# Batch 0's softmax over states computed a second time with tokens on partitions, in a mixed attention and feed-forward kernel on one core

## The chip, the cores and the metric

The kernel runs on 1 core of one Trainium2 chip. The metric is device time in microseconds (us). One execution of each kernel is also taken by the hardware profiler; its trace gives the span and every instruction's start and end. The engines are named as in the trace: PE (TensorE matmul) and PEld (its weight loads), DVE (VectorE), ACT (ScalarE), POOL (GpSimd) and SP (SyncE, which issues most DMAs).

## The reference, cut to what matters

```python
# x: (8, 8, 512, 64) = batch, head, token, width; state: (8, 8, 32, 64)
scores = x @ state.T / 8            # token by state; softmax over the 32 states
xread = softmax(scores) @ state
scores2 = state @ x.T / 8           # state by token; softmax over the 512 tokens
sread = softmax(scores2) @ x
y = concatenate([xread, sread])     # 544 rows of 512 per batch
out = y + relu(layernorm(y) * g @ w_ch1) @ w_ch2      # w_ch1: 512 x 2048
```

Both softmaxes use the same 512 x 32 scores per head, once normalised over the states and once over the tokens.

## The kernel before, in words

Every float32 matrix is split into two float16 halves and each product is made of three or four half products (`TERMS`). The feed-forward part of batch 0 goes directly with the weights, four units of 512 hidden columns; batches 1 to 7 and the state rows go through a Strassen scheme (`products`, lines L895, L905, L953). For each batch, `attention(b)` computes the scores with the states on partitions (a row of the scores tile is one state of one head, its columns are tokens), and from them two things. The softmax over tokens runs along a row: maximum `mB`, exponentials `eB`, their halves `eb`, a DMA transpose to `ebT`, and `read_state` on PE, which gives `sread`. The softmax over states needs the states along the free dimension: `softmax_first` turns the scores in 32 x 32 blocks on DVE (`nc.vector.transpose`, STREAM_TRANSPOSE in the trace) into `ts`, `softmax_rest` subtracts the maximum `mA`, takes the exponential, sums into `dA` and multiplies by the reciprocal, and `numerators` turns the result back on DVE into `ef` and splits it into the halves `ea`. `ea` is the moving operand of the hidden layer's products: `state_products` makes `matrix` (weights times state), and `first_products` (batch 0) multiplies `matrix` with `ea`.

Batch 0 is worked in two parts of 256 tokens (`parts = 2`), and its attention stands among the preparation of the weights: loading, unpacking (`words`: tiles `raw` and `sums`), sums of squares, scales, centring and splitting into `w1c` and `w2h` for four units. That preparation keeps DVE, ACT and POOL occupied and PE partly; PE is given `WARM` = 135 matmuls of ones with ones (`half<-ones`) whose result nobody uses.

The order of all work is written out by hand in `PLAN`: streams of operations are recorded first, and `issue` then emits them in PLAN's order. Each engine runs its own instructions in that order. Stream 177 is the warming matmuls, 1 is `attention(0)`, 2, 7, 12 and 20 are `weights1` of units 0 to 3, 3, 8, 13 and 21 `state_products`, 4, 9, 14 and 22 `first_products`. All recorded operations carry line L187 (the helper `do`), so tiles tell them apart.

PSUM pools matter here: `banks()` is one buffer of two banks (`ps_a`, bufs=1), shared by everything that asks for it (the scores, `read_state`'s result, the next batch's sums of squares and scores); `accumulator()` has four buffers of one bank. In SBUF, `quad` has two buffers, shared by `eB`, `ts`, `ef` and the `part` tiles of batch 0's second layer, which a POOL-issued DMA adds into `xr`.

Of the kernel before, what the change touches and what calls it, by code (L numbers as in the profile page):

```python
# [15 lines left out]
ALU = mybir.AluOpType  # L16
# [144 lines left out]
)  # L161
WARM = 135


class Later:
# [36 lines left out]
def moe_attention(ctx: ExitStack, tc: tile.TileContext, x, state, g_ln, w1, w2, out):  # L202
# [176 lines left out]
    def attention(b):  # L379
# [117 lines left out]
        def softmax_first(s):  # L497
            if b > 0:
                for g in range(G):
                    yield do(scores, g, ps[:, g], sT, xT)  # L500
# [577 lines left out]
```

## Time and profile before

| | us |
|---|---|
| median of 3 runs | 632.14 (631.65 to 632.55) |
| the profiled execution | 632.65 |
| its span | 630.5 |
| PE busy | 614.7 (97% of the span) |
| PEld busy | 483.5 |
| DVE busy | 488.7 (78%) |
| ACT busy | 375.3 (60%) |
| POOL busy | 242.5 (38%) |

The profiled execution has 2.15 us around its span, and is 0.51 us above the median. Busy shares are averages over the whole span: the first 80 us, in which the weights are prepared, and the rest differ.

### The profile page before, as it was taken

What the parts mean: (1) busy time and instruction counts of PE and PEld (TensorE: products, weight loads), DVE (VectorE), ACT (ScalarE), POOL (GpSimd) and SP (SyncE); (2) the same over time, 40 slices, a digit from 0 to 9 for tenths busy, and PEclk for the clock granted to TensorE, in tenths of its full rate; (3) what the DMA queues carried; (4) which work ended last, traced back from release to release, by engine and by line L of the source; (5) the groups of instructions that cost most, each with busy time, mean ns of one, the idle gap of its engine ahead of it and who ended that gap; (6) DMA issues with size and microseconds to landing.
All of it is one profiled execution on the core that took longest, in us unless ns stands there. A gap on an engine that the chain in (4) does not pass through costs nothing.

```text
span 630.5 us, 16626 instructions
## 1 busy us (share of the span) xinstructions
PE 614.7 (97%) x6906; PEld 483.5 (77%) x6906; DVE 488.7 (78%) x1095; ACT 375.3 (60%) x678; POOL 242.5 (38%) x205
## 2 busy tenths in 40 slices
PE   9998998999999999999999999999999999999995
PEld 4355645558888888888888888888878888888884
DVE  4999998898697888688778785889578787564454
ACT  4998988868464844575376454736474544443241
POOL 0011656772262345324433532336224352424132
PEclk9999999999999999999999999999999999999999
DMA  8985293441534143534311246143504025201002
GB/s 289 412 232 191 84 206 68 102 120 43 130 113 120 24 96 68 155 52 132 89 34 39 43 102 156 43 102 50 143 2 77 2 63 145 69 11 25 35 1 68
DMA packets 85355, 62.02 MB, mean 98 GB/s; under 512 B 64608, under 2 KB 77408, under 8 KB 84832
## 3 DMA queue, kind: packets, MB, share of 16 engines
q1 hardware_dynamic: 83008, 57.00, 33.6%
q0 software_dynamic: 864, 3.15, 2.6%
q8 instruction: 54, 0.88, 0.6%
q10 hardware_dynamic: 1408, 0.82, 0.5%
q14 instruction: 21, 0.17, 0.1%
HBM read 28.05 MB, written 9.44 MB: 59 GB/s over the span
## 4 chain that ended last, share of the span: by engine, by line
PE 79%; DVE 13%; ACT 3%; DMA 2%; POOL 1%; issue 1%; DVEq 0%; ACTq 0%
PE acc L953 43%; PE half L895 23%; PE half L905 3%; PE banks L753 3%; DMA xr<-part 2%; PE acc L813 2%; DVE raw L187 2%; DVE x L187 1%; PE half L187 1%; DVE sums L187 1%; DVE w1c L187 1%; PE banks L590 1%; DVE w2h L187 1%; PE banks L472 1%; PE banks L565 1%
## 5 line engine op out<-in xcount | busy, mean ns | idle before, releaser
L953 PEld LDWEIGHTS <-xs 128*128 128x128 f16 x2520 | 244.0, 98 | 34.4 <-issue 6.0
L187 POOL TENSOR_TENSOR xs<-rs,xs 128x512 f16<-128x512 f32 x120 | 144.3, 1212 | 276.4 <-ACT xs L187 195.2
L953 PE MATMUL acc<-w2h,xs 128*128 128x256 f16 x1440 | 182.4, 273 | 0.0
L895 PE MATMUL half<-ea,matrix 128*128 128x256 f16 x1344 | 160.0, 273 | 0.1
L895 PEld LDWEIGHTS <-matrix 128*128 128x128 f16 x1344 | 129.4, 98 | 22.7 <-issue 5.1
L953 PE MATMUL acc<-sums,xs 128*128 128x256 f16 x1080 | 140.7, 273 | 0.0
L187 DVE SCALAR_TENSOR_TENSOR rs<-half,rs 128x256 f32<-128x256 f32 x224 | 90.0, 418 | 43.1 <-ACT rs L187 14.6
L187 ACT ACTIVATE xs<-rs 128x512 f16<-128x512 f32 (+1 forms) x128 | 77.3, 618 | 75.2 <-DVE rs L187 69.0
L187 ACT ACTIVATE xs<-half 128x256 f16<-128x256 f32 (+1 forms) x112 | 53.0, 485 | 58.3 <-PE half L895 30.7
L187 DVE SCALAR_TENSOR_TENSOR xs<-half,xs 128x256 f16<-128x256 f32 (+1 forms) x112 | 60.4, 548 | 24.2 <-ACT xs L187 23.0
L187 POOL TENSOR_TENSOR ts<-ts,mA 128x1024 f32<-128x1024 f32 (+1 forms) x16 | 29.1, 1818 | 55.4 <-DVE mA L187 32.4
L187 ACT ACTIVATE rs<-half 128x256 f32<-128x256 f32 x56 | 21.3, 381 | 39.5 <-PE half L895 32.8
L187 DVE SCALAR_TENSOR_TENSOR matrix<-banks,hs,matrix 128x1024 f16<-128x1024 f32 x28 | 35.8, 1279 | 11.4 <-ACT matrix L187 11.1
L813 PE MATMUL acc<-w2h,hid 128*128 128x512 f16 x192 | 43.2, 379 | 0.2 <-ACT strip L187 0.2
L187 DVE TENSOR_TENSOR strip<-acc,strip 128x256 f32<-128x256 f32 (+1 forms) x60 | 32.9, 549 | 9.1 <-PE acc L953 5.2
L813 PEld LDWEIGHTS <-hid 128*128 128x128 f16 x192 | 18.4, 98 | 23.9 <-issue 3.3
L187 PE MATMUL half<-ones 128*128 128x512 bf16 x135 | 34.9, 402 | 1.1 <-DVE part_mean L358 1.1
L187 ACT ACTIVATE matrix<-banks,hs 128x1024 f16<-128x1024 f32 x28 | 31.1, 1109 | 8.1 <-PE banks L753 8.0
L187 POOL TENSOR_TENSOR hid<-strip,hid 128x512 f16<-128x512 f32 x16 | 21.8, 1369 | 23.2 <-ACT hid L187 23.1
L187 PEld LDWEIGHTS <-ones 128*128 128x128 bf16 x135 | 13.0, 102 | 17.8 <-issue 5.8
L187 DVE SCALAR_TENSOR_TENSOR x<-x_f,x_s,x 128x512 f16<-128x512 f32 x32 | 24.8, 801 | 1.0 <-ACT x L187 0.9
L799 PE MATMUL acc<-ea,matrix 128*128 128x256 f16 x192 | 22.8, 272 | 2.5 <-DVE w1c L187 1.2
(152 smaller groups left out, 756.0 us busy)
## 6 DMA issues: line engine op xcount, KB each, us to landing
raw<-in_moe_w_ch_dram SPq DMA_DIRECT2D x11, 1024.0 KB, 8.5
out_dram<-xr SPq DMA_DIRECT2D x16, 512.0 KB, 3.3
x_f<-in_x_dram SPq DMA_DIRECT2D x14, 512.0 KB, 5.3
sums<-in_moe_w_ch_dram SPq DMA_DIRECT2D x5, 1024.0 KB, 8.0
ek<-ea SPq DMA_DIRECT2D x56, 64.0 KB, 2.0
ek<-ek SPq DMA_DIRECT2D x7, 512.0 KB, 4.2
xr<-part POOLq DMA_DIRECT2D x6, 512.0 KB, 4.6
s_r<-in_state_dram SPq DMA_DIRECT2D x28, 64.0 KB, 3.7
```

The lines of the kernel that those rows point to most:

```text
L187: return lambda: f(*map(now, args), **{k: now(v) for k, v in kw.items()})
L472: nc.tensor.matmul(o[32 * j:32 * j + 32], lhsT=state_of(b, sT, g, j, a), rhs=xT[:, 2 * j + g].rearrange("p c t -> p (c t)"), start=a == 0, ...
L565: nc.tensor.matmul(o[32 * j:32 * j + 32, g], lhsT=ebT[:, e, g, c, 32 * j:32 * j + 32], rhs=xv[:, 2 * j + g, c, i], start=c == 0 and n == 0 ...
L590: nc.tensor.matmul(px[:, c, D * h:D * h + D], lhsT=ek[:, h % 2, h // 2, (2 * t + c) * P:(2 * t + c + 1) * P], rhs=sk[:, h], start=True, st ...
L753: nc.tensor.matmul(ps[g][32 * j:32 * j + 32], lhsT=state_of(b, sT, g, j, i)[r], rhs=w[r, k, j], start=n == 0, stop=n == 2, skip_group_chec ...
L799: nc.tensor.matmul(o[:, 256 * f:256 * f + 256], lhsT=m[:, g, i, P * (q + f):P * (q + f) + P], rhs=ea[:, s, k, g], start=f == 0 and g == 0 ...
L813: nc.tensor.matmul(po, lhsT=hid[:, i, q, c * P:(c + 1) * P], rhs=w[:, j, q], start=first and q == 0 and n == 0, stop=last and q == 3 and n ...
L895: nc.tensor.matmul(ps[:, 256 * q:256 * q + 256], lhsT=m[:, h, i, P * (2 * k + q):P * (2 * k + q) + P], rhs=ea[:, 0, j, h, 256 * g:256 * g ...
L905: nc.tensor.matmul(ps[:, 256 * q:256 * q + 256].rearrange("p (t n) -> p t n", t=2), lhsT=w[:, i, j, fs], rhs=xsT[:, :, x, j], start=q == 0 ...
L953: nc.tensor.matmul(po[o], lhsT=y[:, n, i, o] if o < 2 else x[:, o - 2, n, i], rhs=v[j], start=u == 0 and n == 0 and k == 0 and o in (2, 1, ...
```

## The change

For batch 0 alone the scores are computed twice. `scores_of_tokens` computes them with tokens on partitions: `xT` is the stationary operand (64 rows by 128 tokens) and the state the moving one (32 columns), 64 matmuls for each of the two parts. DVE reduces and subtracts the maximum out of PSUM, so `ts` is made without a DVE transpose. After exponential, sum and division, `turn` brings the weights back to states on partitions with four PE transposes per part into an accumulator bank, and ACT and DVE split that into `ea`. `scores_of_part` still computes the scores with states on partitions, now after both token parts, for the softmax over tokens only. The new scores live in `pst`, a tile of the same one-buffer pool `banks()` as `ps`. The subtraction of part 1 moves from POOL to DVE. For batches 1 to 7 the functions compute what they did.

`PLAN` is written anew from its first entry to its last, and `WARM` is 119 instead of 135.

```diff
-    "1:3 1:2 1:4-5 177:0-19 1:19 1:0 1:7 1:1 177:20-24 1:6 2:0 0:0-1 2:1 1:16 7:1 1:8 7:0 1:25 0:2 1:9-11 1:14 1:12 1:26 "
...
-WARM = 135
+WARM = 119
...
+        pst = banks() if b == 0 else None
         ps = banks()
...
         def softmax_first(s):
-            if b > 0:
+            for g in range(G):
+                yield do(scores, g, ps[:, g], sT, xT)
+            yield do(nc.vector.transpose, ts, ps.rearrange("p g t -> p (g t)"))
+
+        def scores_of_tokens(s, o, sT, xT):
+            for n, (a, i) in enumerate((*TERMS, (1, 1))):
                 for g in range(G):
-                    yield do(scores, g, ps[:, g], sT, xT)
-            else:
-                yield do(scores_of_part, s, psc, sT, xT)
-            if b > 0:
-                yield do(nc.vector.transpose, ts, ps.rearrange("p g t -> p (g t)"))
-            else:
-                yield do(nc.vector.transpose, ts[:, NT * s:NT * s + NT].rearrange("p (g c t) -> p g c t", g=G, c=2),
-                         psc[:, :, :, s].rearrange("p c g t -> p g c t"))
+                    for j in range(4):
+                        for c in range(2):
+                            r = slice(64 * c, 64 * c + 64)
+                            nc.tensor.matmul(o[:, c, g, j], lhsT=xT[r, i, j, g, s], rhs=state_of(b, sT, g, j, a)[r],
+                                             start=s == 0 and n == 0 and g == 0 and j == 0, stop=n == 3, skip_group_check=True)
+
+        def softmax_of_tokens(s):
+            po = pst.rearrange("p c (s g j n) -> p c s g j n", s=parts, g=G, j=4)[:, :, s]
+            yield do(scores_of_tokens, s, po, sT, xT)
+            po = po.rearrange("p c g j n -> p c (g j) n")
...
+            yield do(nc.vector.tensor_reduce, m2, po, AX.X, ALU.max)
+            yield do(nc.vector.tensor_tensor, t4, po, m2.unsqueeze(3).broadcast_to([P, 2, NK // 2, 32]), ALU.subtract)
+            yield do(nc.scalar.activation, cols(ts, s), cols(ts, s), AF.Exp, scale=es)
+            yield do(nc.vector.tensor_reduce, d_, t3, AX.X, ALU.add)
...
+            yield do(nc.vector.reciprocal, m_, m_)
+            engine = nc.vector if s == 0 else nc.gpsimd
+            yield do(engine.tensor_tensor, t3, t3, m_.unsqueeze(2).broadcast_to([P, NK, 32]), ALU.mult)
+
+            def turn(o, t):
+                for c in range(2):
+                    for g in range(G):
+                        nc.tensor.transpose(o[:, g, c], t[:, c, g], idf)
+            pn = accumulator()
+            yield do(turn, pn.rearrange("p (g c t) -> p g c t", g=G, c=2), cols(ts, s).rearrange("p (c g k) -> p c g k", c=2, g=G))
+            hi, lo = (ea[:, s, i].rearrange("p g t -> p (g t)") for i in range(2))
+            yield do(nc.scalar.activation, hi, pn, AF.Copy, scale=SA)
+            yield do(nc.vector.scalar_tensor_tensor, lo, pn, SA, hi, ALU.mult, ALU.subtract)
...
-        for s in range(parts):
-            yield from softmax_first(s)
         if b > 0:
+            yield from softmax_first(0)
             yield do(nc.vector.tensor_reduce, mB, ps, AX.X, ALU.max)
         else:
+            for s in range(parts):
+                yield from softmax_of_tokens(s)
+            for s in range(parts):
+                yield do(scores_of_part, s, psc, sT, xT)
             yield do(nc.vector.tensor_reduce, mB, ps.rearrange("p c (g t) -> p g c t", g=G), AX.XY, ALU.max)
```

Since PLAN is a table of numbers, the built programs show what it moves. On DVE, right after the first scores of batch 0, the program before has these rows (`banks` is the scores' PSUM tile, `sums` and `raw` are weight unpacking; L187 is the helper):

```order
L187 STREAM_TRANSPOSE ts<-banks 128x512
L187 TENSOR_REDUCE mA<-ts 128x16
L187 SCALAR_TENSOR_TENSOR sums<-sums 128x1024
L187 TENSOR_TENSOR ts<-ts,mA 128x512
L187 TENSOR_SCALAR raw<-raw 128x1024
L187 SCALAR_TENSOR_TENSOR sums<-sums 128x1024
L187 STREAM_TRANSPOSE ts<-banks 128x512
L187 TENSOR_REDUCE mA<-ts 128x16
L187 TENSOR_REDUCE dA<-ts 128x16
L346 TENSOR_REDUCE of_columns<-acc 128x1
L187 TENSOR_REDUCE mB<-banks 128x2
```

The changed program has these at the same place (the helper is L186 there):

```order
L186 TENSOR_REDUCE mA<-banks 128x16
L186 TENSOR_TENSOR ts<-banks,mA 128x512
L186 SCALAR_TENSOR_TENSOR sums<-sums 128x1024
L186 TENSOR_REDUCE mA<-banks 128x16
L186 SCALAR_TENSOR_TENSOR sums<-sums 128x1024
L186 TENSOR_REDUCE dA<-ts 128x16
L186 TENSOR_REDUCE mA<-dA 128x16
L186 RECIPROCAL mA<-mA 128x16
L186 TENSOR_TENSOR ts<-ts,mA 128x512
L186 TENSOR_SCALAR raw<-raw 128x1024
```

The two transposes are gone, part 0's weights are finished in one run of rows, and `mB` has left this place: it stands some forty rows later, after unit 1's weights have begun.

The second place is where DVE finishes unit 0's split weights `w1c` and goes over to the first `matrix`. Before:

```order
L187 STREAM_TRANSPOSE ef<-ts 128x512
L187 SCALAR_TENSOR_TENSOR w1c<-acc,of_weights,w1c 128x512 x2
L346 TENSOR_REDUCE of_columns<-acc 128x1
L187 SCALAR_TENSOR_TENSOR w1c<-acc,of_weights,w1c 128x512
L187 SCALAR_TENSOR_TENSOR x_140<-x_f,x_s,x_140 128x8x64
L187 TENSOR_REDUCE dA<-ts 128x16
L187 TENSOR_REDUCE mA<-dA 128x16
L187 RECIPROCAL mA<-mA 128x16
L187 SCALAR_TENSOR_TENSOR ea<-ef,ea 128x512
L187 TENSOR_SCALAR of_weights<-acc,g_98 128x1
L323 TENSOR_SCALAR of_weights<-of_weights 128x1
L187 SCALAR_TENSOR_TENSOR matrix<-acc,matrix 128x512 x2
```

The changed program at the same place:

```order
L186 SCALAR_TENSOR_TENSOR w1c<-acc,of_weights,w1c 128x512 x2
L186 SCALAR_TENSOR_TENSOR raw<-raw 128x1024
L186 SCALAR_TENSOR_TENSOR w1c<-acc,of_weights,w1c 128x512
L186 TENSOR_SCALAR raw<-raw 128x1024
L186 SCALAR_TENSOR_TENSOR raw<-raw 128x1024 x2
L345 TENSOR_REDUCE of_columns<-acc 128x1
L186 SCALAR_TENSOR_TENSOR matrix<-acc,matrix 128x512 x2
```

Batch 0's softmax rows have left the stretch between the last `w1c` and the first `matrix` (part 0's `ea` comes earlier now), and weight unpacking (`raw`) has moved in.

## Rows read from the trace of the kernel before

**Rows 1.** The span in 40 equal slices (15.8 us each): busy share of PE in tenths, and the granted PE clock in tenths of full speed.

```profile
PE   9998998999999999999999999999999999999995
PEclk9999999999999999999999999999999999999999
```

**Rows 2.** Busy time of each engine by stretches of the span (from:to in us, length, then PE, PEld, DVE, ACT, POOL each with its instruction count, then granted PE clock, DMA share, GB/s).

```profile
30.00:40.00 10.00, 9.40 (x165) 4.66 (x164) 9.86 (x20) 10.00 (x14) 1.30 (x1) 1.00 0.76 207
50.00:60.00 10.00, 7.88 (x141) 5.00 (x141) 9.90 (x18) 8.15 (x17) 1.92 (x1) 1.00 0.69 229
140.00:150.00 10.00, 10.00 (x129) 8.01 (x128) 9.29 (x15) 8.61 (x17) 2.02 (x3) 1.00 0.27 72
620.00:630.00 10.00, 3.71 (x35) 3.07 (x32) 3.86 (x7) 0.60 (x1) 0.72 (x1) 0.88 0.27 84
```

**Rows 3.** All that PE waited for in the span, by line and by what released it: us in total, times, longest.

```profile
PE acc L670 <- DVE sums L187: 1.5, 3, 0.5
PE acc L799 <- DVE w1c L187: 1.2, 1, 1.2
PE acc L698 <- ACT part L187: 1.2, 1, 1.2
PE half L187 <- DVE part_mean L358: 1.1, 1, 1.1
PE acc L670 <- DVE w1c L187: 0.9, 1, 0.9
PE acc L799 <- DVE matrix L187: 0.4, 1, 0.4
...
PE acc L813 <- ACT strip L187: 0.2, 1, 0.2
```

**Rows 4.** PE's instructions in order of time, neighbours of one kind merged: start us, us (the last one's end included), what, count, idle before.

```profile
9.49 0.27 PE L351 MATMUL banks<-x_part,ones 128*128 128x1 bf16 x5
9.62 0.64 PE L455 MATMUL acc<-idf,x_f 128*128 128x128 f32 x4
10.09 0.38 PE L412 MATMUL banks<-idf,sh 128*128 128x128 f32 x2
...
15.12 0.87 PE L481 MATMUL banks<-xT,sT 64*32 64x128 f16 x64
...
28.65 4.27 PE L187 MATMUL half<-ones 128*128 128x512 bf16 x19
32.99 1.08 PE L670 MATMUL acc<-raw 128*128 128x128 bf16 x16
33.91 2.10 PE L187 MATMUL half<-ones 128*128 128x512 bf16 x9
...
39.79 2.78 PE L799 MATMUL acc<-ea,matrix 128*128 128x256 f16 x24 [0.41 <-DVE matrix L187]
...
60.73 0.52 PE L605 MATMUL acc<-sh,ea 32*128 32x64 f16 x24
...
69.77 7.93 PE L813 MATMUL acc<-w2h,hid 128*128 128x512 f16 x36 [0.24 <-ACT strip L187]
```

**Rows 5.** Groups of instructions by line, engine, operation and shape in the first 90 us: count, busy us, mean ns of one, idle before.

```profile
L187 PEld LDWEIGHTS <-ones 128*128 128x128 bf16 x132 | 12.7, 102 | 17.7 <-issue 5.8 <-DVE part_mean L358 1.1
L187 DVE STREAM_TRANSPOSE ef<-ts 128x512 f32<-128x512 f32 x2 | 1.4, 710 | 0.0
L187 DVE STREAM_TRANSPOSE ts<-banks 128x512 f32<-128x512 f32 x2 | 1.4, 708 | 0.0
L187 DVE TENSOR_TENSOR ts<-ts,mA 128x512 f32<-128x512 f32 x2 | 1.4, 689 | 0.0
L187 DVE SCALAR_TENSOR_TENSOR ea<-ef,ea 128x512 f16<-128x512 f32 x2 | 1.3, 658 | 0.0
L187 DVE SCALAR_TENSOR_TENSOR xT<-acc,x_s,xT 128x512 f16<-128x512 f32 x4 | 2.8, 746 | 0.0
```

**Rows 6.** DVE's instructions in order of time, in the columns of Rows 4.

```profile
15.24 1.41 DVE L187 SCALAR_TENSOR_TENSOR x<-x_f,x_s,x 128x512 f16<-128x512 f32 x2
...
23.63 1.22 DVE L187 TENSOR_REDUCE mB<-banks 128x2 f32<-128x1024 f32 x1
...
29.65 1.22 DVE L187 SCALAR_TENSOR_TENSOR eb<-eB,eb 128x1024 f16<-128x1024 f32 x1
...
35.68 0.74 DVE L187 SCALAR_TENSOR_TENSOR w1c<-acc,of_weights,w1c 128x512 f16<-128x512 f32 x1
...
37.00 0.68 DVE L187 TENSOR_REDUCE dA<-ts 128x16 f32<-128x512 f32 x1
...
38.96 1.28 DVE L187 SCALAR_TENSOR_TENSOR matrix<-acc,matrix 128x512 f16<-128x512 f32 x2
...
56.95 1.27 DVE L187 SCALAR_TENSOR_TENSOR matrix<-acc,matrix 128x512 f16<-128x512 f32 x2
...
64.73 0.15 DVE L187 TENSOR_SCALAR x_m<-banks 128x2 f32<-128x2 f32 x1
```

**Rows 7.** The chain that ended last, in order of time, between 60 and 135 us: start us, us, what.

```profile
81.28 1.29 DVE w2h L187
...
82.66 1.26 POOL raw L187
...
87.54 8.38 DMA xr<-part
```

More of the change, by code (lines that the diff above doesn't have):

```diff
@@ new lines, in softmax_of_tokens @@
+        def softmax_of_tokens(s):
+            po = pst.rearrange("p c (s g j n) -> p c s g j n", s=parts, g=G, j=4)[:, :, s]
+            yield do(scores_of_tokens, s, po, sT, xT)
+            po = po.rearrange("p c g j n -> p c (g j) n")
+            t3 = cols(ts, s).rearrange("p (k n) -> p k n", n=32)
+            t4 = cols(ts, s).rearrange("p (c k n) -> p c k n", c=2, n=32)
+            m_, d_ = (v[:, NK * s:NK * s + NK] for v in (mA, dA[:, 0]))
+            m2 = m_.rearrange("p (c k) -> p c k", c=2)
+            yield do(nc.vector.tensor_reduce, m2, po, AX.X, ALU.max)
+            yield do(nc.vector.tensor_tensor, t4, po, m2.unsqueeze(3).broadcast_to([P, 2, NK // 2, 32]), ALU.subtract)
+            yield do(nc.scalar.activation, cols(ts, s), cols(ts, s), AF.Exp, scale=es)
+            yield do(nc.vector.tensor_reduce, d_, t3, AX.X, ALU.add)
+            yield do(nc.vector.tensor_reduce, m_, dA[:, 0:2, NK * s:NK * s + NK].rearrange("p two k -> p k two"), AX.X, ALU.add)
+            yield do(nc.vector.reciprocal, m_, m_)
[10 more added lines that the diff above has]
+            yield do(nc.vector.scalar_tensor_tensor, lo, pn, SA, hi, ALU.mult, ALU.subtract)
@@ L509, in softmax_rest @@
         def softmax_rest(s):
-            engine = nc.vector if b == 0 and s == 0 else nc.gpsimd
+            engine = nc.gpsimd
             t3 = cols(ts, s).rearrange("p (k n) -> p k n", n=32)
@@ L549, in attention @@
         yield columns(2, rB, rB, isx, 1.0 / SE, ALU.mult, ALU.mult)
-        for s in range(parts):
-            yield from softmax_rest(s)
-        if b == 0:
+        if b > 0:
+            yield from softmax_rest(0)
+        else:
             for q in range(4):
@@ L570, in attention @@
         yield do(nc.vector.tensor_tensor, sread, pr, rB.unsqueeze(2).broadcast_to([P, G, D]), ALU.mult)
-        for s in range(parts):
-            yield from numerators(s)
+        if b > 0:
+            yield from numerators(0)
         if b > 0:
```

242 rows, old and new, of the table PLAN are left out of this document.

## Prediction

> **What bounds the kernel now.** I read the page's slices first, then the busy time by stretches, then all waits of PE, then the order in time of PE and DVE in the first 80 us, then the chain that ended last.
>
> [...] By stretches it is finer: from 140 us on PE is busy for 10.00 of 10 us, while between 30 and 40 us DVE has 9.86 and ACT 10.00, and between 50 and 60 us PE falls to 7.88 with DVE at 9.90 [rows 2]. So there are two regimes. In the preparation of the weights DVE and ACT are full and PE is filled up with warming matmuls; afterwards PE is the bound. PE waits in 13 places, 8.2 us in all (the seven rows shown are 6.5 of it) [rows 3]; all of them lie before 140 us, since PE is full from there, and the rest of PE's idle time is the tail. The end therefore moves by two things only: the PE work in its queue ahead of about 140 us, and the sum of its waits there. After that, and in the tail (PE 3.71 of the last 10 us [rows 2]), the rewritten order has the same instructions and ends with the same rows, so I cost it at nothing. What hides it is PE's own full queue: DVE and ACT have 0.7 and 1.4 us free in 140 to 150 us [rows 2], and where that cover were gone each wait would cost its own length.
>
> **The change, on PE.** It adds 128 token-score matmuls, each with its own load of 64 rows by 128 columns and only 32 moving columns. No such instruction is in the trace. Below, the old scores run 64 in 0.87 us, 13.6 ns each, but with loads of 32 columns; above, the 128 x 128 Gram products take 0.92 us for 16, 57.5 ns each, with 128 moving columns [rows 4]. The nearest rows are those with loads of 128 columns and few moving ones: L605 with 24 in 0.52 us, 22 ns, and L351 with a full load and one column, 5 in 0.13 us, 26 ns [rows 4]. I take 23 ns: 128 x 0.023 = 2.9 us, with ends of 1.7 and 7.4 us. It adds 8 transposes; the turns of x, also float32 128 x 128, run four in 0.47 us [rows 4], so 8 x 0.118 = 0.9 us. It takes away 16 warming matmuls, 19 of which run in 4.34 us [rows 4]: 16 x 0.228 = 3.7 us. The queue of PE is as long as before within 0.1 us, by the ends -1.1 to +4.6.
>
> [...]
>
> **The change, on DVE.** Four 32 x 32 transposes go, 0.71 us each, one subtraction comes from POOL, 0.69 us, and the two lower halves of `ea` read PSUM: 0.75 against 0.66 us [rows 5]. That is -2.8 + 0.7 + 0.2, so -1.9 us of work on an engine that is full. POOL loses one subtraction, which costs and gives nothing since it waits there. ACT keeps its count.
>
> The new order moves more than that. Up to the fourth `w1c` of unit 0 DVE loses three transposes (2.1), two `x` rows (1.4), `mB` with its columns (1.5), `eb` (1.2) and one column maximum (0.3); it gains part 1's subtraction, part 0's `ea` and part 1's `dA` (0.7 each) and two small rows (0.4) [rows 5, 6]. That is -6.5 + 2.5 = -4.0 us. Against it stand two new waits. Token scores of part 0 can start when `xT` is complete, where the old ones started, at 15.12 [rows 4], and take 1.5 us; DVE, which went on with `x` at 15.24 [rows 6], now has nothing from about 15.8 and waits 0.8. Part 1's scores write the same PSUM tile as part 0's, so they wait for DVE's subtraction of part 0 and are done 1.5 us after it, while DVE has one 1.1 us row to do: 0.4. Queued behind both waits on DVE is everything for `w1c`. Net -2.8: the row that ends at 36.4 [rows 6] ends near 33.6.
>
> Then DVE has 3.4 us of unpacking before the first `matrix`, which ends near 38.3 instead of 40.2, 2 us early. By the same count over both orders DVE's queue is 5.2 us shorter at the second `matrix` (58.2 [rows 6]) and 3.4 us at the last `w2h` half of the chain, at 81.28; less the 1.2 of waits that leaves 4.0 and 2.2. That last row matters: POOL starts its differences after it, and behind them issues the accumulation into `xr`, which takes 8.38 us [rows 7] and frees a `quad` buffer for ACT's next `part`. With 2.2 us at its head this chain also moves early by 2.2.
>
> **What PE's waits become.** At the start 1.1 stays. Ahead of the token scores 0.3 and 0.1. Before unit 0's state product PE has done its fillers at about 32.4 and waits for `w1c` at 33.6 to 33.9: 1.4. Before unit 1's, 0.4. Before the next batch's sums of squares 0.5, since those come later on ACT. The five waits after 69 us are 2.4 (part of [rows 3]) and I leave them. Sum 6.2 against 8.2: what goes is mostly the waits for `w1c` and `sums` between 18 and 53 us. So PE gives -2.0, DVE's chain -2.2; the smaller decides. The profiled execution of 632.65 (span 630.5 and 2.15 around it) becomes 630.65; it lies 0.51 above the median of 632.14, so the forecast for the median is **630.1 us**.
>
> **Rivals.**
>
> *No change: the waits stay.* The token scores, the state scores, `read_state` and the next batch's sums of squares all go through the one `banks` buffer, now one user more. `read_state` and `sread` come later, and only then can batch 1's `x_m` be formed, which stood at 64.73 [rows 6]; by my count it is 0.6 us later while all else is early. If batch 1's attention then sets when PE becomes full, the waits return to 8.2 and the time is 632.14 + 0.1 = 632.2. For it: 16 fewer fillers is about what the new PE work takes, as if the room had only been refilled. Against it: no wait of PE in the rows is for batch 1's scores.
>
> *Slower: the token scores cost like the Gram products.* At 57.5 ns [rows 4] PE has 4.5 us more, and each half takes 3.7 us instead of 1.5, so DVE, in order, waits 2.2 us more twice, ahead of all `w1c`. The gain of 2.0 turns into a loss of about 2.0 to 2.5: 634.4. It decides from 0.023 + 2.0/128, about 39 ns each. For it: these have as many weight columns as the Gram products. Against it: the 22 and 26 ns rows.
>
> *Slower by far: loads one after another.* A load lasts 102 ns in the trace [rows 5]. Were the 128 loads not overlapped, they would take 13.1 us, 10.2 more than I count: about 640. The 26 ns row speaks against it. [...]
>
> [...]
>
> *More is gained.* With 13.6 ns a token score and half of the remaining early waits gone, -1.2 and -3.7: 627.2.
>
> **Chances.** Forecast (631.2 to 628) 0.52; no change 0.27; slower through the token scores 0.12; serial loads 0.02; the clock 0.02; more gained 0.05. A measurement of this kernel tells about 0.2%, 1.3 us, from no change; a little of the forecast's own spread falls inside that. Faster 0.53, same 0.31, slower 0.16. For 8 in 10 the range leaves out most of the larger gain and of the slower cases: 627.6 to 633.2. The likeliest case alone would be 628.3 to 631.5.
>
> **What would show it.** 64 token scores in 1.4 to 1.7 us right: the PE term; 3 us or more: the slower rival. Four turns in 0.5 us. The fourth `w1c` near 33.9, unit 0's first products near 38 instead of 39.8, the first second-layer products near 68 instead of 69.8 [rows 4], the accumulation into `xr` issued near 85. PE's waits at 6 us; 8 or more says that the room was refilled. A wait of PE after 145 us, or one for `banks` in batch 1's attention, would make the forecast wrong; so would a granted clock below its upper level.

## The result, and the profile after

The change makes the kernel slower: 637.15 us (four runs, 636.16 to 637.89) against 631.89 us, a ratio of 1.0087 with a 95% interval of 1.0075 to 1.0099. The forecast was 630.1, with a range up to 633.2, so it was wrong in sign and outside its range. The profiled execution took 636.16 us with a span of 634.2; before, the span was 630.5, so the two profiles differ by 3.7 us. That is the distance that the traces can explain; the medians stand further apart because the profile of before lies 0.8 us above its median and that of after 1.0 below.

PE still looks full in the slices, and the granted clock shows nine nearly everywhere. They answer [rows 1]:

```profile
PE   9799998998999999999999999999999999999995
PEclk9999999999999999999999999999999999999998
```

What the slices hide is in the waits of PE, which answer [rows 3] (line, tile, releaser, then us in total, times, longest):

```profile
PE banks L481 <- issue: 3.4, 1, 3.4
PE acc L985 <- POOL xs L186: 2.5, 1, 2.5
PE acc L350 <- DVE of_columns L345: 1.4, 1, 1.4
PE banks L785 <- DVE matrix L186: 1.4, 1, 1.4
PE half L186 <- DVE part_mean L357: 1.1, 1, 1.1
```

The waits sum to about 11.5 us where they were 8.2. The two longest are new, and behind each of them the granted clock fell. In these stretches of the kernel after (columns as in [rows 2]) the column behind the POOL counts is the granted clock:

```profile
25.00:30.00 5.00, 1.74 (x20) 0.69 (x20) 4.96 (x10) 5.00 (x7) 0.00 (x1) 0.88 1.02 400
30.00:35.00 5.00, 5.00 (x26) 2.32 (x25) 4.90 (x7) 5.00 (x6) 1.04 (x1) 0.78 1.02 415
145.00:150.00 5.00, 3.26 (x38) 1.99 (x39) 2.64 (x4) 2.93 (x4) 3.37 (x3) 0.83 0.37 112
150.00:155.00 5.00, 5.00 (x40) 4.18 (x39) 3.41 (x6) 1.01 (x2) 1.15 (x1) 0.83 0.00 0
```

All other stretches up to 160 us show 1.00. Read in steps of 0.1 us the clock is 1.00 or 0.50 in these stretches: 0.50 from 28.8 to 32.2 us and from 148.3 to 151.7, 3.4 us each time, and 1.00 around them. These two are the upper and the lower level below. PE's own rows show what ran there (L508 are the token scores, L531 the turns, L481 the state scores; columns as in [rows 4]):

```profile
14.23 0.96 PE L508 MATMUL banks<-sT,xT 64*128 64x32 f16 x64
15.13 1.47 PE L186 MATMUL half<-ones 128*128 128x512 bf16 x6
...
21.59 0.66 PE L531 MATMUL acc<-idf,ts 128*128 128x128 f32 x4
...
23.57 1.26 PE L481 MATMUL banks<-xT,sT 64*32 64x128 f16 x113
28.27 0.33 PE L481 MATMUL banks<-xT,sT 64*32 64x128 f16 x15 [3.43 <-issue]
28.52 5.10 PE L186 MATMUL half<-ones 128*128 128x512 bf16 x15
...
40.49 1.47 PE L831 MATMUL acc<-ea,matrix 128*128 128x256 f16 x12
...
68.47 3.72 PE L845 MATMUL acc<-w2h,hid 128*128 128x512 f16 x16
...
146.74 0.61 PE L985 MATMUL acc<-w2h,xs 128*128 128x256 f16 x4 [2.54 <-POOL xs L186]
147.28 0.84 PE L785 MATMUL banks<-w1c,sT 64*32 64x512 f16 x24
148.05 1.30 PE L985 MATMUL acc<-sums,xs 128*128 128x256 f16 x6
149.15 2.71 PE L985 MATMUL acc<-w2h,xs 128*128 128x256 f16 x12
```

After 113 of its 128 state scores PE stops for 3.43 us and is released by nothing that the profile shows. The 15 warming matmuls behind it take 4.94 us from the first start to the next kind of row (at 33.46), where 15 take 3.34 at a granted clock of 1.00 (24.99 to 28.33 in the run with the scores in two pieces, below). Then, at 146.74, PE waits 2.54 us for `xs` from POOL, and of the products behind it 18 take from 148.05 to 151.70, 3.65 us instead of 1.97 (145.56 to 147.53 in the first run below).

In between the kernel is ahead. The first-layer products start at 40.49 against 39.79 [rows 4], late because of the stop, but the second-layer products start at 68.47 against 69.77 [rows 4], 1.3 us ahead (0.7 of it only because `x_f` landed earlier in this execution: the second turns of x start at 8.93 instead of 9.62 [rows 4]). At 131.56, the first Strassen product, the lead is 0.1, so without the early `x_f` none is left. By 152 us the 2.54 of the wait and 1.7 of the lower clock have come on top, PE is full from there in both kernels, and the last row of PE starts 3.6 us later than before. So the profile leaves two things to explain: the stop at 24.8 us, and the wait at 144.2.

POOL's rows give a first answer for the second (columns as above):

```profile
138.90 1.27 POOL L186 TENSOR_TENSOR raw<-raw 128x512 f32<-128x512 f32 x1
143.42 1.70 POOL L186 TENSOR_TENSOR sums<-sums 128x512 f32<-128x512 f32 x1 [3.25 <-DVE sums L186]
145.09 1.60 POOL L186 TENSOR_TENSOR xs<-rs,xs 128x512 f16<-128x512 f32 x1
```

POOL is idle for 3.25 us with a subtraction at the head of its queue that waits for DVE; the `xs` row that PE needs stands behind it. ACT had finished the other half of that `xs` at 139.71, so `xs` could have run from 140.2. In PLAN the subtraction is item 19:3 (the last difference of unit 2's `sums_of_weights`). It stood 107 items ahead of this `xs` (29:14) in the old list; in the new one it stands directly ahead of it, and behind the DVE item it waits for.

### The profile page after: what moved, and what is told of

It reads as the page before. It is cut to its first block, busy times and chain, and to the rows that moved or that the text cites. A ratio compares the mean times of both kernels' runs of the same rounds, so it can differ in the third digit from the quotient of the medians.

```text
span 634.2 us, 16869 instructions
## 1 busy us (share of the span) xinstructions
PE 615.3 (97%) x7026; PEld 485.6 (77%) x7026; DVE 484.8 (76%) x1092; ACT 376.6 (59%) x678; POOL 239.0 (38%) x204
## 4 chain that ended last, share of the span: by engine, by line
PE 83%; ACT 8%; POOL 3%; DVE 3%; issue 2%; DMA 1%; ACTq 0%; POOLq 0%; DVEq 0%
PE acc L985 44%; PE half L927 23%; PE half L937 3%; PE banks L785 3%; PE half L186 2%; PE acc L845 2%; ACT sums L186 2%; PE banks L622 1%; POOL raw L186 1%; PE banks L472 1%; PE banks L597 1%; ACT strip L186 1%; DVE sums L186 1%; DMA xr<-part 1%; ACT hid L186 1%
## 5 line engine op out<-in xcount | busy, mean ns | idle before, releaser
L186 POOL TENSOR_TENSOR xs<-rs,xs 128x512 f16<-128x512 f32 x120 | 141.5, 1192 | 265.2 <-ACT xs L186 186.6
L927 PE MATMUL half<-ea,matrix 128*128 128x256 f16 x1344 | 161.9, 273 | 0.1
L186 DVE SCALAR_TENSOR_TENSOR rs<-half,rs 128x256 f32<-128x256 f32 x224 | 90.3, 416 | 44.0 <-ACT rs L186 21.8
L186 ACT ACTIVATE xs<-rs 128x512 f16<-128x512 f32 (+1 forms) x128 | 76.9, 618 | 68.9 <-DVE rs L186 66.0
L186 ACT ACTIVATE xs<-half 128x256 f16<-128x256 f32 (+1 forms) x112 | 53.7, 485 | 70.4 <-PE half L927 27.6
L186 DVE SCALAR_TENSOR_TENSOR xs<-half,xs 128x256 f16<-128x256 f32 (+1 forms) x112 | 60.6, 549 | 26.4 <-ACT xs L186 25.1
L186 POOL TENSOR_TENSOR ts<-ts,mA 128x1024 f32<-128x1024 f32 (+1 forms) x15 | 28.7, 1913 | 52.3 <-DVE mA L186 46.5
L186 DVE TENSOR_TENSOR strip<-acc,strip 128x256 f32<-128x256 f32 (+1 forms) x60 | 32.7, 544 | 16.0 <-PE acc L985 11.1
L186 ACT ACTIVATE rs<-half 128x256 f32<-128x256 f32 x56 | 21.3, 380 | 39.1 <-PE half L927 33.4
L186 DVE SCALAR_TENSOR_TENSOR matrix<-banks,hs,matrix 128x1024 f16<-128x1024 f32 x28 | 35.7, 1275 | 7.7 <-ACT matrix L186 7.6
L186 ACT ACTIVATE matrix<-banks,hs 128x1024 f16<-128x1024 f32 x28 | 31.1, 1109 | 11.3 <-PE banks L785 8.2
L186 POOL TENSOR_TENSOR hid<-strip,hid 128x512 f16<-128x512 f32 x16 | 20.4, 1299 | 43.2 <-ACT hid L186 43.2
L186 PE MATMUL half<-ones 128*128 128x512 bf16 x119 | 31.9, 415 | 1.1 <-DVE part_mean L357 1.1
L785 PE MATMUL banks<-w1c,sT 64*32 64x512 f16 x672 | 23.6, 379 | 1.4 <-DVE matrix L186 1.4
L186 DVE BATCH_NORM_STATS2 s<-xr 128x6 f32<-128x512 f32 x32 | 21.5, 680 | 4.2 <-ACT xr L186 4.2
L186 DVE SCALAR_TENSOR_TENSOR x<-x_f,x_s,x 128x512 f16<-128x512 f32 x32 | 23.1, 760 | 1.3 <-ACT x L186 1.3
```

The lines of the kernel that those rows point to most:

```text
L186: return lambda: f(*map(now, args), **{k: now(v) for k, v in kw.items()})
L785: nc.tensor.matmul(ps[g][32 * j:32 * j + 32], lhsT=state_of(b, sT, g, j, i)[r], rhs=w[r, k, j], start=n == 0, stop=n == 2, skip_group_chec ...
L927: nc.tensor.matmul(ps[:, 256 * q:256 * q + 256], lhsT=m[:, h, i, P * (2 * k + q):P * (2 * k + q) + P], rhs=ea[:, 0, j, h, 256 * g:256 * g ...
```

## Experiments

All medians below were measured beside the kernel before: 631.67 us for the first four, 632.03 for the other three. The edits to PLAN are written as stream:item.

**The late wait: POOL's subtraction behind `xs`.**

```diff
-28:5 19:3 29:14 30:2 19:10-11
+28:5 29:14 19:3 30:2 19:10-11
```

> One POOL instruction changes places in the changed kernel: the last subtraction of the third unit's weight sums (sums<-sums, at 143.42 us in the profile after) goes behind the low half of the hidden activations (xs, at 145.09) instead of ahead of it. Theory A, the late wait: TensorE's 2.54 us wait at 146.74 for xs is POOL's order, and the granted clock of 0.91 to 0.92 from 145 to 152 us follows from that wait. Then the wait is gone, the clock stays at its upper level, and 2.5 us of wait and about 1.7 us of clock go: 637.1 - 4.2 = 632.9 us. Rival: ACT and DVE are as late, so that another wait of TensorE takes its place within the next 5 us: 636 to 637 us.

Measured 631.63 us (ten runs, 630.91 to 632.40), ratio to before 0.9991 (0.9969 to 1.0013). The span is 630.0, 4.2 us shorter than that of the changed kernel, which is what theory A had from the rows; the medians differ by 5.5. POOL's and PE's rows of this run:

```profile
139.12 1.27 POOL L186 TENSOR_TENSOR raw<-raw 128x512 f32<-128x512 f32 x1
140.35 1.16 POOL L186 TENSOR_TENSOR xs<-rs,xs 128x512 f16<-128x512 f32 x1
143.65 1.71 POOL L186 TENSOR_TENSOR sums<-sums 128x512 f32<-128x512 f32 x1 [2.14 <-DVE sums L186]
```

```profile
144.04 0.82 PE L985 MATMUL acc<-w2h,xs 128*128 128x256 f16 x6
144.79 0.84 PE L785 MATMUL banks<-w1c,sT 64*32 64x512 f16 x24
145.56 0.83 PE L985 MATMUL acc<-sums,xs 128*128 128x256 f16 x6
146.22 1.47 PE L985 MATMUL acc<-w2h,xs 128*128 128x256 f16 x12
```

The subtraction still starts when DVE lets it, at 143.65, and nobody minds. PE's six products run at 144.04 without a wait, and the granted clock is 1.00 from 145 to 155 us (the 0.91 to 0.92 of the expectation are the means of 140 to 150 and 150 to 160 us in the changed kernel). One POOL instruction in the wrong place was the whole of the late loss in the trace, and the rival (another wait within 5 us) falls. The stop of 3.48 us at the state scores is still there in this run.

**The early stop: the state scores in two pieces.** Item 1:51 is the second 64 of them.

```diff
-1:44 1:51 2:26 20:3 2:23 10:2 2:20 10:3 1:45 177:53-67 7:8
+1:44 2:26 20:3 2:23 10:2 2:20 10:3 1:45 177:53-67 1:51 7:8
```

> In the changed kernel the second 64 state scores go behind the 15 warm-up products that follow them, nothing else moves. Theory B, instructions: TensorE stopped for 3.43 us after 113 of 128 state scores because the next instructions had not arrived; each product and each weight load is one instruction, and 256 of them were used up in 1.6 us. Then it would stop at the same number in its list of instructions, which here stands after 98 of the 128 (the 15 warm-up products stand for 30 rows), but gets there only near 28 us, when they are there: wait 0 to 0.5 us instead of 3.4, no lower granted clock from 28 to 33 us, first-layer products near 38 instead of 40.5 us. The time then falls by up to the 2.7 us that DVE waits for TensorE at 37.8 and 40.7 us: 634.4 us, with the late wait of 2.5 us still there. Rival C: the wait belongs to the scores themselves (their bank or their operands): they wait as long behind the warm-up products: 637 us.

Measured 634.20 us (632.34 to 635.22), ratio 1.0044 (1.0027 to 1.0061): 2.95 us under the changed kernel, with the late wait of 2.5 us still there; its four runs lie 2.9 us apart. PE's rows:

```profile
24.24 0.81 PE L481 MATMUL banks<-xT,sT 64*32 64x128 f16 x64
24.99 3.41 PE L186 MATMUL half<-ones 128*128 128x512 bf16 x15
28.33 0.49 PE L481 MATMUL banks<-xT,sT 64*32 64x128 f16 x34
28.98 0.44 PE L481 MATMUL banks<-xT,sT 64*32 64x128 f16 x30 [0.17 <-issue]
...
38.09 1.47 PE L831 MATMUL acc<-ea,matrix 128*128 128x256 f16 x12
```

What is left of the stop, 0.17 us, comes after 64 + 15 + 34 = 113 products, the very place in PE's list where it stood before, although another instruction stands there now. So the stop goes with a place in the list and not with the scores, as theory B says. The counts agree, in a list of another order too: when PE stops without a releaser it has started 349 products and 350 loads in the changed kernel, in the POOL run, here and in the filled run below, and 350 of each in the first two old-order runs below, where the next product is a `gm` one. The transfers agree as well. The profile of the changed kernel has one queue of kind instruction whose 0.90 MB are 64 bytes for each of PE's 14,052 loads and products, in 55 packets:

```profile
q8 instruction: 55, 0.90, 0.6%
```

One packet, 16 KB, is then some 256 instructions, by estimate from these numbers. Between 16 and 30 us this queue moved two, one at 18.15 and one at 25.80, and PE went on 2.47 us after the second. In the run above it went on 2.58 after it (26.40 to 28.98), in the POOL run 2.58 (25.90 to 28.48), in the filled run below 2.55 (25.65 to 28.20), in the two old-order runs that stop 2.34 (25.45 to 27.79) and 2.30 (25.35 to 27.65). That the queue is PE's, and that PE waits for its packets, is inferred from the bytes and the times; that PE goes on 2.3 to 2.6 us after the packet, in six runs, is measured. The kernel before has such a packet at 25.75 too, but starts its 700th load or product only at 38.3 us, and does not stop. The granted clock stays at 1.00 from 25 to 35 us here.

This trace also limits what may be said of the clock at the late wait. PE waits the same 2.54 us for `xs`, and the clock stays up behind it (first PE's row, then the stretch, granted clock behind the POOL count):

```profile
144.54 0.61 PE L985 MATMUL acc<-w2h,xs 128*128 128x256 f16 x4 [2.54 <-POOL xs L186]
145.00:150.00 5.00, 5.00 (x64) 3.98 (x63) 2.88 (x5) 2.10 (x3) 1.16 (x1) 1.00 0.01 3
```

So behind the same wait the clock fell in one execution (0.83 from 145 to 155 us) and not in another (1.00 from 145 to 150), and the spans of two single traces differ by that too: of the 3.9 us between this one (630.3) and the changed kernel's, 1.7 are the late clock and not the stop.

**Both edits.**

> Both edits: the POOL subtraction behind xs, and the second 64 state scores behind the 15 warm-up products. Theories A and B together: 637.1 - 4.2 - 2.7 = 630.2 us, 1.7 under the kernel before. Rival: from 50 us on DVE and ACT set the pace, and what is gained early is given back as waits before 125 us: as the POOL edit alone, 632.9 us.

Measured 629.59 us (628.95 to 630.89), ratio 0.9971 (0.9958 to 0.9984): faster than both kernels, by 2.1 us than the one before. Span 626.9. Rows of PE, then its longest waits:

```profile
37.13 1.47 PE L831 MATMUL acc<-ea,matrix 128*128 128x256 f16 x12
...
65.61 4.59 PE L845 MATMUL acc<-w2h,hid 128*128 128x512 f16 x20
```

```profile
PE acc L350 <- DVE of_columns L345: 1.4, 1, 1.4
PE banks L785 <- DVE matrix L186: 1.4, 1, 1.4
PE half L186 <- DVE part_mean L357: 1.1, 1, 1.1
PE acc L702 <- DVE acc L186: 1.1, 1, 1.1
```

The early gain is not given back: this run is 2.0 us under the POOL edit alone, a second price of the stop beside the 2.95 above. The rival falls, though the spreads of the runs leave the size open by about 1 us.

**The wait filled instead of removed.** What is the lower clock worth by itself? Item 27:6 is the state product that stood behind the wait.

```diff
-30:2 19:10-11 31:6 47:3 31:10 27:6 30:1
+27:6 27:6 27:6 30:2 19:10-11 31:6 47:3 31:10 30:1
```

> The changed kernel with the wait at 146.7 us filled instead of removed: the 24 products of the next state product (0.84 us, they stood right behind the wait) are put ahead of it and are computed three times over (the same result each time; 1.6 us of work that nothing needs). POOL's order stays. Theory F, the lower clock after the wait is a price of its own, beside the wait: with TensorE busy through the wait the granted clock stays at its upper level from 145 to 152 us, and the 18 products behind it take 1.96 us instead of 3.65. The filled wait itself gives 0.95 us (its 0.84 us of needed work, and the four products behind it at the upper level). Time 637.1 - 0.95 - 1.7 = 634.5 us. Rival: the clock falls there for another reason: 636.2 us and still 0.9 from 145 to 152 us.

Measured 635.02 us (ten runs, 632.99 to 636.22), ratio 1.0049 (1.0034 to 1.0064); span 631.8, 2.4 less than the changed kernel (2.1 by the medians), where theory F has 2.65 and the rival 0.95.

```profile
143.22 2.14 PE L785 MATMUL banks<-w1c,sT 64*32 64x512 f16 x72
...
146.73 0.61 PE L985 MATMUL acc<-w2h,xs 128*128 128x256 f16 x4 [0.40 <-POOL xs L186]
147.17 0.82 PE L985 MATMUL acc<-sums,xs 128*128 128x256 f16 x6
147.83 1.47 PE L985 MATMUL acc<-w2h,xs 128*128 128x256 f16 x12
```

PE reaches the `xs` products no earlier than in the changed kernel (146.73 against 146.74), but the 18 products behind them take 1.97 us, and the granted clock reads 1.00 from 145 to 155 us. So in the changed kernel's trace the lower clock was a price of its own behind the idle 2.54 us, about 1.7 us, and here, with 1.6 us of useless work in the wait, it is not paid. Since the clock also stayed up once behind the unfilled wait (the run with the scores in two pieces), one trace does not show that the filling did it. The single runs speak for it: their mean granted clock over the span is 0.994 to 0.997 in these ten and 0.991 to 0.994 in the four of the changed kernel.

**The new softmax in the old order.** Every other item stands where it stood before, with 135 warming matmuls; the new parts take the places of those that they replace, the turns those of the old transpositions. One piece of the list shows the manner (39 to 41: second token scores, their maximum, their subtraction; 50 and 51: the state scores):

```diff
-2:8 1:30 10:1 1:43 7:6 1:44 2:7 7:5 177:52-53 2:9 1:31 1:49 1:45 2:10
+2:8 1:39 10:1 1:30 7:6 1:31 2:7 7:5 177:52-53 2:9 1:40 1:32 1:41 1:50-51 2:10
```

> The new softmax in the old order: every work item of the kernel before stands where it stood (135 warm-up products too); the parts of the new softmax take the places of those that they replace, each turn that of the old transposition, and the state scores stand right behind the second subtraction. Theory D, the order costs and not the softmax: no wait after 140 us as before; 128 token scores at 14 ns (1.8 us) and 8 turns (1.0 us) come on top of TensorE's list, DVE's 1.9 us go: 631 to 633 us. Rival E, the new work costs it wherever it stands: 635 us or more.

Measured 647.98 us, ratio 1.0257 (1.0242 to 1.0272). Theory D, as it was put, is refuted: the old order is far from free. PE stands still in front of the first turn, and DVE behind it:

```profile
39.61 1.11 PE L531 MATMUL acc<-idf,ts 128*128 128x128 f32 x4 [4.34 <-DVE ts L186]
```

```profile
48.11 0.29 DVE L345 TENSOR_REDUCE of_columns<-acc 128x1 bf16<-128x128 f32 x1 [7.01 <-PE acc L702]
```

A transposition on DVE that waits for `ts` holds up DVE, which is the engine that makes `ts`. A turn on PE that waits for `ts` holds up the Gram products behind it, and for them DVE then waits 7.01 us. Besides, the granted clock falls to 0.64 from 20 to 25 us and is 0.50 from 25 to 30. PE's waits sum to 16.3 us (8.2 before), and PE is busy for 622.3 us (614.7 before). But rival E (the new work costs it wherever it stands) does not follow either, since the same work in the new order runs in 629.59. The run with the first turn moved behind the Gram products:

```diff
-1:35-36 177:66-84 7:8 2:24 2:30 7:9-10 2:21 10:5 1:69 1:43 177:85-93 3:0
+1:35 177:66-84 7:8 2:24 2:30 7:9-10 2:21 10:5 1:69 1:43 177:85-93 3:0 1:36
```

> The new softmax in the old order, as the run before, with one TensorE item moved: the first four turns, at which TensorE waited 4.34 us for DVE's ts (39.61 us), stand behind the 19 + 9 warm-up products, the Gram products and the first state product that followed them. Theory G, a turn in TensorE's queue makes the old order dear, because what stands behind it waits too (the Gram products, on which DVE waited 7.0 us): 648.0 less 4.3 of wait and 1.0 to 3 of lower clock behind it = 641 to 643 us. Rival: DVE's chain to the fourth w1c is what is late, and TensorE waits elsewhere for the same result: 646 to 648 us.

Measured 644.21 us, ratio 1.0193 (1.0167 to 1.0219): 3.8 us better, about what the wait itself was, and no more. Between the two expectations: theory G has the mechanism right for this one wait, but the rest of the old order is as late. What makes up the other 12 us was not taken apart; PE's waits still sum to 14.3 us here, and the granted clock is 0.50 from 25 to 30 us.

```profile
PE acc L831 <- DVE ea L186: 3.7, 1, 3.7
PE acc L702 <- DVE sums L186: 2.4, 2, 2.0
```

PE now waits 3.7 us for `ea`, and the clock falls there instead (0.66 from 50 to 60 us). The last run of this line also parts the state scores:

```diff
-1:50-51 2:10 2:16 7:2-3 1:52 177:54-55 2:11-12
+1:50 2:10 2:16 7:2-3 177:54-55 1:51-52 2:11-12
```

> As the run with the turns moved, and the second 64 state scores stand five work items later, behind two warm-up products, just ahead of the maximum that reads them. Theory B, instructions: TensorE's 2.07 us wait at 27.79 us gets shorter only by what TensorE does before it, some 0.5 us, since the list's place is reached early either way; 640.5 to 642.5 us. Rival, the 128 state scores in one piece make the wait: it goes, 639 to 641 us.

Measured 643.44 us, ratio 1.0206 (1.0156 to 1.0256), not to be told from the run before it. The stop (1.9 us in the run before) went entirely, which I had given to the rival. But it decides nothing: the second piece started at 28.95, later than I had reckoned, and the packet had come at 25.90, so by theory B too (2.3 to 2.6 us after it) nothing was left to wait for: PE starts its 700th load or product only at 29.6 us.

## Why the prediction was wrong

**The step that failed first** is the sentence that costs all after 140 us at nothing, because "the rewritten order has the same instructions and ends with the same rows" and PE's full queue hides the rest. PE's queue was full from 140 us before, and that is a property of the old order, not of the work. The sum looked at the end of the two lists and at the first 90 us, and not at POOL's rows at the hand-over to the Strassen part, where `sums<-sums` now stands between the two `xs`. That one row cost 4.2 us by the spans (5.5 by the medians). The text named the sign of it (a wait after 145 us, a granted clock below the upper level), and gave the fall of the clock 2 in 100. No run shows what makes the clock fall. What the runs showed is a clock of 0.50 for 3.4 us behind the stop of 3.43 us and for 3.4 us behind the wait of 2.54, and 1.00 behind the same wait in another run.

**The second step that failed** is that the state scores were moved at no cost. They have the same 128 products as before, but not in two pieces of 64 with other work between them. In one piece, and behind 256 new loads and products of the token scores, they bring PE in 1.26 us to a place in its list whose instructions, by theory B, have not come (the packet is there at 25.80, PE at 24.8). The forecast priced the new and the moved small products by their time on PE alone. The stop of 3.43 us and the 1.6 us of clock behind it cost the end 2.95 us by the medians, 2.0 between the POOL run and the run with both edits; part of the rest was covered, since without the stop PE waits 0.82 and 0.37 us for DVE at the same place. No rival had this mechanism.

**With both undone the time is 629.59**, 0.5 from the 630.1 of the forecast. That does not make the sum right: its waits gained half of what was forecast, and the shorter PE list, which it had at nothing, made up for it by luck. Its terms are these.

- *Token scores*: 23 ns each were forecast, 14 were measured (64 from 14.23 to 15.13). The lower end, 13.6, was nearly right, since the number of weight columns hardly mattered here (14 ns with 128 of them, 12.5 to 13.6 with 32); 1.8 us in place of 2.9. The Gram-price rival and the serial loads fall. The trace has 92 ns for each of these loads, 5.9 us for 64 one after another, but 64 pairs of load and product took 0.90 us, so the loads overlap. The recorded length hardly goes with the columns: the loads of 32 columns have 90 ns.
- *Turns*: 0.49 us for four, from 21.59 to 22.08, as forecast. *Warming*: 15 in 3.3 us at a granted clock of 1.00, 0.22 each, as forecast. So PE's queue is 0.8 us shorter, not 0.1 longer.
- *DVE up to the fourth `w1c`*: 33.6 to 33.9 was forecast. It starts at 32.13 and ends at 32.88:

```profile
32.13 0.75 DVE L186 SCALAR_TENSOR_TENSOR w1c<-acc,of_weights,w1c 128x512 f16<-128x512 f32 x1
...
37.83 0.29 DVE L345 TENSOR_REDUCE of_columns<-acc 128x1 bf16<-128x128 f32 x1 [1.90 <-PE acc L702]
38.04 1.28 DVE L186 SCALAR_TENSOR_TENSOR matrix<-acc,matrix 128x512 f16<-128x512 f32 x2
```

  0.7 of that is the early `x_f`; net of it the end, 33.6, is the forecast's, but by another sum. DVE's busy time up to this row fell by 3.5 us (28.09 to 24.55) and not by 4.0. The two new waits of 0.8 and 0.4 that I had put against the gain do not exist: small rows stand in the first, an unpacking row covers the second; 0.5 is waited ahead of `sT` (11.02) instead. The first `matrix` then starts at 38.04 only because DVE waits 1.90 us for Gram products behind PE's stop. In the run with both edits first-layer products start at 37.13 (forecast 38) and second-layer products at 65.61 (forecast 68); there the second turns of x start at 8.70, 0.9 us earlier than before, so net of it they are at 38.1 and 66.5.
- *The chain through POOL into `xr`* was to be issued near 85 instead of 87.54 [rows 7]. It was issued at 91.11: the new order puts four `raw` differences (84.91, 6.26 us) ahead of it. DVE's head start of 1.0 us (its `w2h` row at 80.30 against 81.28) did not matter, and neither did the delay, since the next accumulations were no later (96.22 against 96.46).
- *PE's waits*: 6.2 forecast, 11.5 measured, 7.3 with both edits. The five after 69 us that I left at 2.4 became 3.6 up to 132 us: 1.41 for `of_columns` at 105.3 and 1.35 for `matrix` at 130.8 are others than before. That is where the lead of 1.3 us at 68 us went. What the kernel with both edits gains comes less from the waits (8.2 to 7.3) than forecast, and more from the shorter PE list (0.8).

The rival "no change" and its `banks` argument did not decide, but it was not empty. No wait of PE in batch 1's attention is for that buffer; the 1.35 us at 130.8 are. There a state product of batch 1 waits to write `banks` until DVE has read the one before it (`matrix<-banks`, 129.50 to 130.74), and DVE had stood 1.21 us for POOL's `ts`. The wait of this kind before was 0.31 us (137.39).

## What to carry to other kernels

A price of nothing for a stretch that is full now holds only for the order that made it full: where a list is rewritten, compare every engine's rows at each hand-over, and above all what stands ahead of the row that the bound engine needs next in a queue that runs in order. Work moved from DVE to PE takes its wait with it and holds up what stands behind it there; such a move needs a new order around it (16 us slower in the old one, 4 of them by one such wait), and the new order is then part of what is measured. Before a rewritten order is judged, remove its longest single waits: here two moves of one item each turned 0.9% slower into 0.3% faster.

## What the runs showed of the hardware

- PE stopped without a releaser in the profile. In a run of 128 loads and 128 products, 113 pairs of them in 1.26 us, it stopped for 3.43, 3.48 and 2.98 us in three runs, and for 1.9 and 2.1 us in two of the old order. Around the stop of the changed kernel the 16 DMA engines' share was 1.06 and 1.02 (365 and 400 GB/s from 20 to 25 and 25 to 30 us). The stop comes after 349 or 350 products and 350 loads, whatever work stands there, and ends 2.3 to 2.6 us after a 16 KB packet on an instruction queue (six runs, with the 0.17 us of the scores in two pieces). That PE waits there for its instructions is inferred. Whether the busy DMA engines make the packet late, or it would come as late without them, was not tried.
- Token scores with 64 x 128 loads and 32 moving columns run at 14 ns a pair, little slower than those with 64 x 32 loads and 128 moving columns (12.5 to 13.6).
- The wait of 2.54 us at 144 us was followed by a granted clock of 0.50 (148.3 to 151.7 us) that cost 1.7 us more, the stop of 3.43 us by one (28.8 to 32.2 us) that cost 1.6; with the wait filled or removed the clock read 1.00. But behind the same wait of 2.54 us in the run with the scores in two pieces it read 1.00, as it did after the waits of 1.41 and 1.35 us at 105 and 131 us; in the first old-order run it fell at 21.4 us, in a wait of 1.99 us. So the length of one wait does not decide it, and what does was not found.
